# Inverse-FFT tail of a fused attention + spectral kernel: accumulating the second group's product in PSUM, stores ahead of loads on the SP queue, turned rows eight partitions apart

## The chip, the cores and the metric

The kernel runs on one core of one Trainium2 chip. The metric is the device time of one execution in microseconds (us), lower is better. The time before the change is the median of three executions.

## The reference

The network interleaves two kinds of residual block, twice: attention, spectral filter, attention, spectral filter. All tensors are float32, with 2048 rows and 1024 columns.

```python
def _A_ref(x, wqkv, wo):                      # 32 heads of 32 columns
    qkv = (x @ wqkv).reshape(B, S, 3, H, Dh).transpose(2, 0, 3, 1, 4)
    q, k, v = qkv[0], qkv[1], qkv[2]
    p = softmax(einsum("bhqd,bhkd->bhqk", q, k) * Dh ** -0.5)
    return einsum("bhqk,bhkd->bhqd", p, v).transpose(0, 2, 1, 3).reshape(B, S, D) @ wo

def _B_ref(x, w_r, w_i):
    X = rfft2(x, axes=(-2, -1)) * (w_r + 1j * w_i)
    return irfft2(X, s=(S, D), axes=(-2, -1))

x = A_x
x = x + _A_ref(_layernorm(x), A_wqkv, A_wo)
x = x + _B_ref(_layernorm(x), B_w_r, B_w_i)
x = x + _A_ref(_layernorm(x), A_wqkv, A_wo)
x = x + _B_ref(_layernorm(x), B_w_r, B_w_i)
```

## The kernel before

`build` calls, for each of two layers, `attention` and then `spectral`. Here layer 0 and layer 1 mean these two passes. The change lies in the last two parts of `spectral`, which run once in each layer, so everything told below happens twice in one execution: about 1645 to 1857 us (layer 0, followed by the attention of layer 1) and about 3490 to 3710 us (layer 1, followed by nothing).

`spectral` computes the two-dimensional FFT, the product with the weights and the inverse FFT as chains of matmuls. Its middle part works on 32 *units* (`UNITS`, units 0 to 15 in group g = 0, units 16 to 31 in group g = 1; four column blocks each, in a few units five). For each unit i there are these steps:

- `fb(i)`: 12 matmuls (forward transform along the rows) into PSUM, then `restack` on ScalarE copies them into the tile B (L1115).
- `fc(i)`: 8 matmuls, then four VectorE products with the weights w (L1161 to L1164) and two GpSimd adds (L1168, L1169). At its end `loadw(i + 3)` issues the load of a later unit's weights from the SP queue (L1089), and the weights are prepared on GpSimd (L1101).
- `halves(i)`: a copy on ScalarE (L1179) and a subtraction on VectorE (L1180) that make the float16 tile H.
- `binv(i)`: 12 matmuls with H, then `restack` into U on ScalarE.
- `cinv(i)`: 8 matmuls with U (L1199), a ScalarE copy into T, a tile with three buffers (L1204), and a *store* of T, 256 KB, to `zt[i]` in DRAM from the SP queue (L1205).
- `turn(i)` for even i: a *load* of 512 KB from `zt[i:i + 2]` back into SBUF, from the SP queue (L1209). It exchanges partitions and columns: two units make 16 rows of 64 x 128 float32, each row is one partition of the tile `turned`. `row(i, r, j)` says which partition a row lies in; the 16 rows of a turn are neighbours, `8 * (i % 16)` to `8 * (i % 16) + 15`. The constant matrix `mi` is laid out by the same function.

The loop over i runs 36 iterations as a software pipeline: iteration i does `fb(i)`, `halves(i - 2)`, `fc(i - 1)`, `binv(i - 3)`, for odd i from 7 on `turn(i - 7)`, then `cinv(i - 4)`, then for odd i the load of 128 rows of y, 512 KB, into `rest` (L1235). In this loop the order of the instructions on TensorE, ScalarE and SP is the order in which they are written (`manual_schedule`); the other engines, and everything where no such block stands, are ordered by the framework's planner. After the loop comes `turn(30)`. A turn waits for the stores of its two units. All of these DMAs are issued from one queue, SP, in order: an instruction there that waits holds up whatever stands behind it.

The last part applies the remaining inverse transform of length 16 and adds the result to the residual. For each of eight column blocks a, `even(a)` multiplies group 0 (`ai(a, 0)`, 8 matmuls of 128x128x128 float32, L1248, in the trace 16 instructions) and `odd(a)` multiplies group 1 (`ai(a, 1)`). Call the products p0 and p1, each a PSUM tile of two banks; four such tiles exist (`pq`). The residual has two halves, x0 and x1, and the result is x0 + p0 + p1 and x1 + p0 - p1. Before the change this is done so: ScalarE copies p0 to an SBUF tile e (L1257), VectorE adds p0 to x0 (L1258), VectorE subtracts p1 from e (L1265), VectorE adds p1 to x0 (L1266), GpSimd adds e to x1 (L1267). For the last block a = 7 one half of the columns is done by VectorE alone (L1274). The order is even(0) to even(3), then odd(0), even(4), odd(1), even(5), and so on.

In layer 0 this part also runs the first weight preparations of the next attention (`nxt`): eight loads of 256 KB from SP (L312), splits on ScalarE and VectorE (L218, L219) for v and on ScalarE and GpSimd (L321 to L323) for k and q. It also computes statistics for the coming layernorm (L1288, and `tile_root` in the middle of block 7). The next attention starts with a normalisation on ScalarE (L380) whose scale and bias come from `tile_root`. In layer 1 each finished block a is stored to the output, 1 MB each (L1292, and L1295 in two halves for the last).

Of the kernel before, what the change touches and what calls it, by code (L numbers as in the profile page):

```python
# [6 lines left out]
F32 = mybir.dt.float32  # L7
# [4 lines left out]
AF = mybir.ActivationFunctionType  # L12
ALU = mybir.AluOpType
# [9 lines left out]
UNITS = [u for g in range(2) for u in  # L23
         [(g, k1, list(range(4 * h, 4 * h + 4))) for k1 in range(1, 8) for h in range(2)]
         + [(g, k1, [0, 1, 2, 3] if g else [1, 2, 3, 0, 4]) for k1 in (0, 8)]]
# [4 lines left out]


def row(i, r, j):
    return 8 * (i % 16) + 2 * j + r


def spec_consts():
# [74 lines left out]
NG, NCH, NKT, NST = 8, 4, 16, 6  # L111
# [9 lines left out]
def ln_pow(nc, sm, cst, mv, eng, n=1):  # L121

    v, r = (sm.tile([128, n], F32, name=f"{c}{n}") for c in "vr")
    eng.tensor_scalar(v, mv[:, 1::2], 1e-5, None, op0=ALU.add)
    nc.gpsimd.tensor_tensor(r, v, cst["mhalf"].broadcast_to([128, n]), op=ALU.pow)
    return v, r


def ln_root(nc, sm, mv, v, r, eng, m=1.0):

    q, s, b = (sm.tile([128, 1], F32, name=f"{c}1") for c in "qsb")
    eng.scalar_tensor_tensor(q, r, r, v, op0=ALU.mult, op1=ALU.mult)
    eng.scalar_tensor_tensor(s, q, -3.0, r, op0=ALU.add, op1=ALU.mult)
    last = eng.scalar_tensor_tensor(b, mv[:, 0:1], 0.5 * m, s, op0=ALU.mult, op1=ALU.mult)
    eng.tensor_scalar(r, s, -0.5, None, op0=ALU.mult)
    return r, b, last
# [21 lines left out]
def tile_stats(nc, ap, flags, layer, t):  # L158
    if layer and t < NST:
        st = flags["st"][:, t]  # L160
        nc.vector.bn_stats(st[:, 1], ap.x[:, t, 512:1024])
    else:
        st = bn_stats(nc, ap.sm, ap.x[:, t])
    mv = flags["mv"][:, layer * 16 + t]
    nc.vector.bn_aggr(mv, st)
    return mv


def tile_root(nc, ap, cst, flags, layer, t):

    mv = tile_stats(nc, ap, flags, layer, t)
    v, r = ln_pow(nc, ap.sm, cst, mv, nc.vector)
    yield
    r, b, flags["pin"] = ln_root(nc, ap.sm, mv, v, r, nc.vector)
    flags["rb"] = r, b
    yield
# [827 lines left out]
def spectral(nc, tc, ap, yd, xout, a, cst, zt, fast, flags=None, nxt=None, join=None):  # L1004
# [25 lines left out]
    turned = ap.r.rearrange("p (g q n) -> p g q n", g=2, q=64)  # L1030
    rest = ap.big.rearrange("p (t d) -> p t d", d=1024)
    xo = rest.rearrange("p t (a u g q) -> p g a t u q", a=8, g=2, q=8)
# [84 lines left out]
    def complex_mm(out, lr, li, c):  # L1117

        sel = ((0, 0),) if parts == 1 else ((0, 0), (0, 1), (1, 0))
        mm_ = [(l[x], c[y][:, o:o + 256]) for l, o in ((lr, 128), (li, 0)) if l is not None for x, y in sel]  # L1120
        for k, (l, r) in enumerate(mm_):
            nc.tensor.matmul(out, l, r, start=k == 0, stop=k == len(mm_) - 1)  # L1122

    def const(n, k1):
        return [C[n][:, k1, y] for y in range(2)] if fast else [C[n][:, k1]]

    def new_ps(n):
        return [ps.tile([128, 2, 2, 128], F32, name="ps") for _ in range(2 if n == 5 else 1)]
# [47 lines left out]
    def halves(i):  # L1176
        while todo and todo[0][0] == i:
            _, gs, hi, lo = todo.pop(0)
            nc.scalar.copy(hi, gs)  # L1179
            nc.vector.tensor_sub(lo, gs, hi)  # L1180

    def binv(i):
        g, k1, fs = UNITS[i]
        n = len(fs)
        G = Gt.pop(i)
        pb = new_ps(n)
        for j, o, m in PAIRS[n]:
            lr, li = ([v[:, r, o:o + m].rearrange("p a f -> p (a f)") for v in G] for r in range(2))
            complex_mm(pb[j // 2][:64 * m, j % 2].rearrange("p r k -> p (r k)"), lr, li, const("cbi", k1))
        U = Ut[i] = p2.tile([128, 6, 128], F32, name="U")  # L1190
        restack(n, pb, U)

    def cinv(i):
        g, k1, fs = UNITS[i]
        n = len(fs)
        U = Ut.pop(i)
        pt = ps.tile([128, 4, 128], F32, name="ps")
        for j in range(4 if n == 4 else 3):
            nc.tensor.matmul(pt[:, j], C["ci"][:, 8 * g + fs[j]], U[:, j], start=True, stop=True)  # L1199
        if n == 5:  # L1200
            for j in range(2):
                nc.tensor.matmul(pt[64 * j:64 * j + 64, 3], C["ci"][:, 8 * g + fs[3 + j], 0:64], U[:, 4 + j], start=True, stop=True)
        t_ = p4.tile([128, 4, 128], F32, name="T")
        nc.scalar.copy(t_, pt)  # L1204
        nc.sync.dma_start(zt[i].rearrange("j p n -> p j n"), t_)  # L1205

    def turn(i):
        r0 = row(i, 0, 0)
        nc.sync.dma_start(turned[r0:r0 + 16, UNITS[i][0]],  # L1209
                          zt[i:i + 2].rearrange("i j (r q) n -> (i j r) q n", q=64))  # L1210

    for i in range(lead):
        loadw(i)
# [1 line left out]
    with tc.manual_schedule(engines=set(hold)) if fast else nullcontext():  # L1215
        for i in range(36):
            if i < 32:
                fb(i)
            if 0 <= i - 2 < 32 and fast:
                halves(i - 2)  # L1220
            if 0 <= i - 1 < 32:
                fc(i - 1)
            if 0 <= i - 3 < 32:
                binv(i - 3)
            if 7 <= i and i % 2:
                turn(i - 7)
            if 0 <= i - 4 < 32:
                cinv(i - 4)
            if i == 20 and join:
                joined = join(ps)  # L1230
            if 20 <= i < 23 and join:
                next(joined, None)
            if i % 2 and i < 32:
                t = i // 2
                nc.sync.dma_start(rest[:, t], yd[t * 128:(t + 1) * 128, :])  # L1235
        turn(30)
    psum.close()
    work.close()
    mid.close()
# [2 lines left out]
    psum = Pools(tc, None)  # L1242
    pq = psum("ai_ps", 4, space=PSUM)

    def ai(a, g):
        p = pq.tile([128, 8, 128], F32, name="ai")
        for q in range(8):
            nc.tensor.matmul(p[:, q], turned[:, g, 8 * a + q], cst["mi"][:, g], start=True, stop=True)  # L1248
        return p.rearrange("p q (t u) -> p t u q", u=8)

    def even(a):
        p = ai(a, 0)
        e = ap.pp.tile([128, 8, 128], F32, name="e", tag="p")
        ev = e.rearrange("p q (t u) -> p t u q", u=8)
        x0 = xo[:, 0, a]
        h = 8 if a < 7 else 4
        nc.scalar.copy(e[:, :h], p.rearrange("p t u q -> p q (t u)")[:, :h])  # L1257
        nc.vector.tensor_add(x0[:, :, :, :h], x0[:, :, :, :h], p[:, :, :, :h])  # L1258
        return p, e, ev

    def odd(a, p0, e, ev):
        p = ai(a, 1)
        x0, x1 = xo[:, 0, a], xo[:, 1, a]
        h = 8 if a < 7 else 4
        nc.vector.tensor_sub(e[:, :h], e[:, :h], p.rearrange("p t u q -> p q (t u)")[:, :h])  # L1265
        nc.vector.tensor_add(x0[:, :, :, :h], x0[:, :, :, :h], p[:, :, :, :h])  # L1266
        nc.gpsimd.tensor_tensor(x1[:, :, :, :h], x1[:, :, :, :h], ev[:, :, :, :h], op=ALU.add)  # L1267
        if a == 7:
            m, k = (iter(()), 8) if flags is None else (tile_root(nc, ap, cst, flags, 1, 0), 1)
            with tc.manual_schedule(engines={mybir.EngineType.DVE}):  # L1270
                for t in (slice(0, k), slice(k, 16)):
                    for n, (v, y, op) in enumerate(((x0, p0, ALU.add), (x1, p0, ALU.add), (x0, p, ALU.add),
                                                    (x1, p, ALU.subtract))):
                        nc.vector.tensor_tensor(v[:, t, :, h:], v[:, t, :, h:], y[:, t, :, h:], op=op)  # L1274
                        if n == (1 if t.start else 3):
                            next(m, None)

    first = [even(a) for a in range(4)]
    for a in range(8):
        odd(a, *first.pop(0))  # L1280
        if a < 4:
            first.append(even(a + 4))
        if nxt is not None:
            for _ in range(2):
                next(nxt, None)
            if 4 <= a < 4 + NST // 2:
                for t in range(2 * a - 8, 2 * a - 6):
                    nc.vector.bn_stats(flags["st"][:, t, 0], ap.x[:, t, 0:512])  # L1288
        else:
            sl = slice(a * 128, a * 128 + 128)  # L1290
            if a < 7:
                nc.sync.dma_start(xout[:, sl].rearrange("(t p) d -> p t d", p=128), ap.x[:, :, sl])  # L1292
            else:
                for t, q in ((0, nc.sync), (8, nc.scalar)):
                    q.dma_start(xout[t * 128:t * 128 + 1024, sl].rearrange("(t p) d -> p t d", p=128), ap.x[:, t:t + 8, sl])  # L1295
    if nxt is not None:
        run(nxt)
    psum.close()
# [224 lines left out]
```

## Time and profile before

| what | value |
|---|---|
| time, median of 3 executions | 3707.57 us (3706.04 to 3711.98) |
| time of the profiled execution | 3711.67 us |
| its span, first to last instruction | 3709.8 us |
| TensorE busy | 3606.5 us (97%) |
| VectorE busy | 3128.7 us (84%) |
| ScalarE busy | 2899.0 us (78%) |
| GpSimd busy | 664.0 us (18%) |
| 32 units of layer 0, first `fb` to last store | about 1645 to 1808 us |
| last part of layer 0 (L1248 to the next attention's first L380) | 1801 to 1856 us |
| last part of layer 1 | 3645 to 3710 us |

The busy shares are averages over the whole span, of which the spectral parts are about a tenth. Rows of the profile name an engine (PE is TensorE, PEld its weight loads, DVE VectorE, ACT ScalarE, POOL GpSimd, SPq the SyncE queue), a line of the kernel, the operation and the tiles. Since SBUF is swapped between the layers, `turned` and `rest` appear under the names of the buffers they lie in: in layer 0 `turned` is R and the residual is big, in layer 1 `turned` is big and the residual is R.

### The profile page before, as it was taken

The page shows a single profiled execution, that of the slowest core. Times are in us where ns is not written, and L with a number is a line of the kernel's source. Part 1 is how long each engine was busy: PE and PEld are TensorE (multiplying, and loading weights), DVE is VectorE, ACT ScalarE, POOL GpSimd, SP SyncE. Part 2 cuts the span into 40 slices and gives each one's busy share as a digit, 9 for nine tenths or more (in the row PEclk, how much of TensorE's full clock was granted, in tenths as well). Part 3 has the DMA queues.
Part 4 walks back from the last instruction along what each step waited for, and adds up shares of the span by engine and source line. Part 5 has one row for each costly group of instructions (what it writes and reads, how often), then busy time and mean ns, then how long its engine had stood idle before and what let it go on. Part 6 is the DMA issues. An engine that isn't in the chain of part 4 may idle for free.

```text
span 3709.8 us, 80239 instructions
## 1 busy us (share of the span) xinstructions
PE 3606.5 (97%) x32663; PEld 1595.9 (43%) x32663; DVE 3128.7 (84%) x3754; ACT 2899.0 (78%) x3571; POOL 664.0 (18%) x802
## 2 busy tenths in 40 slices
PE   8999999999999999999699999999999999999995
PEld 5333433343343333388663334334433433333895
DVE  7799899989998989886558998999899889788754
ACT  5788888888888967768448888888888888686783
POOL 1022112211221110024410111111111111000243
PEclk9999999999999999999899999999999999999998
DMA  7122232222232442139651232223222334322497
GB/s 198 21 53 54 52 55 52 56 47 55 47 64 54 97 109 78 69 129 209 151 162 22 55 60 49 55 48 61 41 53 55 64 58 99 100 77 74 137 213 185
DMA packets 238283, 307.71 MB, mean 83 GB/s; under 512 B 77392, under 2 KB 156752, under 8 KB 236368
## 3 DMA queue, kind: packets, MB, share of 16 engines
q1 hardware_dynamic: 198944, 228.49, 22.3%
q0 software_dynamic: 37632, 73.43, 13.7%
q8 instruction: 257, 4.21, 0.5%
q14 instruction: 122, 1.00, 0.1%
q10 hardware_dynamic: 1328, 0.59, 0.1%
HBM read 165.65 MB, written 135.20 MB: 81 GB/s over the span
## 4 chain that ended last, share of the span: by engine, by line
PE 84%; DVE 4%; DMA 4%; issue 4%; ACT 3%; POOL 1%; SPq 0%; DVEq 0%; ACTq 0%; POOLq 0%
PE o L746 24%; PE s L736 20%; PE x L426 16%; PE x L484 7%; PE x L547 6%; PE s L547 3%; DMA zt<-T 2%; PE ps L1122 2%; PE ps L1053 1%; PE ps L1038 1%; DVE acc L759 1%; PE ai L1248 1%; PE o L426 1%; DMA w<-in_w 1%; PE ps L1154 1%
## 5 line engine op out<-in xcount | busy, mean ns | idle before, releaser
L740 ACT ACTIVATE p<-s,bias 128x1024 f32<-128x1024 f32 x2048 | 2169.0, 1111 | 460.1 <-PE s L736 440.8
L759 DVE TENSOR_TENSOR acc<-acc,p 128x1024 f32<-128x1024 f32 x896 | 1044.6, 1223 | 55.8 <-ACT p L740 54.8
L759 DVE TENSOR_TENSOR big<-big,p 128x1024 f32<-128x1024 f32 x448 | 522.7, 1222 | 38.3 <-ACT p L740 37.1
L759 DVE TENSOR_TENSOR R<-R,p 128x1024 f32<-128x1024 f32 x448 | 522.5, 1223 | 31.4 <-ACT p L740 30.0
L746 PE MATMUL o<-p,R 128*32 128x512 f32 x4096 | 492.6, 598 | 0.0
L746 PE MATMUL o<-p,big 128*32 128x512 f32 x4096 | 492.5, 598 | 0.0
L426 PEld LDWEIGHTS <-wqk 128*128 128x128 f16 x3072 | 275.6, 98 | 419.8 <-issue 127.2
L426 PE MATMUL x<-R,wqk 128*128 128x512 f16 x1440 | 338.1, 381 | 1.9 <-ACT big L488 1.2
L426 PE MATMUL x<-big,wqk 128*128 128x512 f16 x1440 | 338.3, 381 | 1.4 <-ACT R L488 0.7
L736 PEld LDWEIGHTS <-R 32*128 32x128 f16 x6144 | 115.2, 93 | 370.5 <-issue 313.0
L736 PEld LDWEIGHTS <-big 32*128 32x128 f16 x6144 | 114.6, 93 | 370.3 <-issue 312.5
L746 PEld LDWEIGHTS o<-p,R 128*32 128x32 f32 x4096 | 107.2, 109 | 261.5 <-issue 261.5
L746 PEld LDWEIGHTS o<-p,big 128*32 128x32 f32 x4096 | 107.1, 109 | 261.5 <-issue 261.5
L736 PE MATMUL s<-R 32*128 32x512 f16 x3072 | 214.1, 378 | 0.1
L736 PE MATMUL s<-Q,big 32*128 32x512 f16 x3072 | 212.8, 378 | 1.0 <-DVE mqk L460 1.0
L736 PE MATMUL s<-Q,R 32*128 32x512 f16 x3072 | 212.7, 378 | 1.0 <-DVE mqk L460 1.0
L736 PE MATMUL s<-big 32*128 32x512 f16 x3072 | 212.8, 378 | 0.5 <-ACT p L740 0.4
L765 POOL DMA_DIRECT2D zd<-acc x112 | 92.3, 825 | 658.5 <-DVE z L775 308.6
L484 PE MATMUL x<-wv,big 128*128 128x256 f16 x1392 | 165.4, 275 | 3.2 <-DVE R L219 2.2
L484 PEld LDWEIGHTS <-big 128*128 128x128 f16 x1536 | 145.4, 98 | 49.1 <-issue 28.9
L484 PE MATMUL x<-wv,R 128*128 128x256 f16 x1392 | 165.7, 275 | 0.7 <-ACT R L392 0.7
L484 PEld LDWEIGHTS <-R 128*128 128x128 f16 x1536 | 145.6, 98 | 46.8 <-issue 26.1
(524 smaller groups left out, 4139.3 us busy)
## 6 DMA issues: line engine op xcount, KB each, us to landing
zd<-acc POOLq DMA_DIRECT2D x112, 256.0 KB, 4.1
wst<-in_wp SPq DMA_DIRECT2D x96, 256.0 KB, 3.5
zt<-T SPq DMA_DIRECT2D x64, 256.0 KB, 8.8
w<-in_w SPq DMA_DIRECT2D x60, 256.0 KB, 7.1
zd<-R POOLq DMA_DIRECT2D x56, 256.0 KB, 4.2
zt<-zr SPq DMA_DIRECT2D x224, 64.0 KB, 2.6
od<-ohl SPq DMA_DIRECT2D x56, 256.0 KB, 2.4
zd<-big POOLq DMA_DIRECT2D x56, 256.0 KB, 4.1
```

The source lines that it names most:

```text
L426: nc.tensor.matmul(ps, a, b, start=i == 0, stop=i == 23)
L484: nc.tensor.matmul(ps[:, j], x[c][:, d, o:o + 128], w[:, n, d], start=i == 0, stop=i == 23)
L547: nc.tensor.matmul(p, a, b, start=start and d == ds[0] and i == 0, stop=stop and d == ds[-1] and i == 2)
L736: nc.tensor.matmul(s[h // 2][:, h % 2], K[g][r, a, kt * 128:kt * 128 + 128], Q[g][r, b, c * 512:c * 512 + 512], start=i == 0, stop=i == 2)
L740: nc.scalar.activation(p, s[hf], AF.Exp, bias=bias[g], scale=SCALE / (SQ * SQ))
L746: nc.tensor.matmul(O[g, c][32 * h:32 * h + 32], V[g][:, kt, 32 * h:32 * h + 32], P[g, c, kt, h // 2][:, h % 2], start=kt == 0, stop=kt == ...
L759: last_add = nc.vector.tensor_add(a, a, p)
L765: nc.gpsimd.dma_start(z, a[32 * j:32 * j + 32].rearrange("p a j n -> p (a j n)"), max_dma_last_dim=2048, **({"accum_op": ALU.add} if j els ...
L1038: nc.tensor.transpose(pt[:, j], xv[:, g, :, 4 * i + j], ident)
L1053: nc.tensor.matmul(pa[:, j], tt[:, x, j], mm[:, g, y], start=k == 0, stop=k == 2)
L1122: nc.tensor.matmul(out, l, r, start=k == 0, stop=k == len(mm_) - 1)
L1154: nc.tensor.matmul(pc[:, j].rearrange("p r f -> p (r f)"), B[:, POS[n][o + j]], C["cc"][:, 8 * g + fs[o + j]], start=True, stop=True)
```

## The change

It has five parts.

1. `row` places the 16 rows of a turn eight partitions apart: turn i goes to partitions c, c + 8, ..., c + 120 with c = i % 16 // 2. `mi` follows by the same function.
2. In the loop `cinv(i - 4)` is written ahead of `turn(i - 7)`, so that on SP the store of unit i - 4 stands ahead of the turn. With the last iterations: before, SP has turn 26, store 29, store 30, turn 28, store 31, turn 30; after, it has store 29, turn 26, store 30, store 31, turn 28, turn 30.
3. `odd(a)` accumulates onto the PSUM tile of `even(a)` instead of using one of its own. Only the first matmul in each bank starts an accumulation. `even(a)` now only makes e = 2 p0 on ScalarE and adds it to x1 on GpSimd. `odd(a)` is two VectorE operations on p = p0 + p1: x0 += p and x1 -= p. The separate treatment of half of block 7 is gone.
4. TensorE and VectorE follow the written order in the last part: even(0) to even(3), odd(0), odd(1), even(4), odd(2), even(5), odd(3), even(6), odd(4), even(7), odd(5), odd(6), odd(7).
5. The first loads and splits of the next attention's weights (those called at a = 0) are issued only after `turn(30)`.

```diff
 def row(i, r, j):
-    return 8 * (i % 16) + 2 * j + r
+    return 8 * (8 * (i % 2) + 2 * j + r) + i % 16 // 2
...
     def turn(i):
         r0 = row(i, 0, 0)
-        nc.sync.dma_start(turned[r0:r0 + 16, UNITS[i][0]],
-                          zt[i:i + 2].rearrange("i j (r q) n -> (i j r) q n", q=64))
+        return nc.sync.dma_start(turned[r0:r0 + 121:8, UNITS[i][0]],
+                                 zt[i:i + 2].rearrange("i j (r q) n -> (i j r) q n", q=64))
...
             if 0 <= i - 3 < 32:
                 binv(i - 3)
+            if 0 <= i - 4 < 32:
+                cinv(i - 4)
             if 7 <= i and i % 2:
                 turn(i - 7)
-            if 0 <= i - 4 < 32:
-                cinv(i - 4)
...
-        turn(30)
+        back = turn(30)
...
+    tiles = {}
+
     def ai(a, g):
-        p = pq.tile([128, 8, 128], F32, name="ai")
+        if g == 0:
+            tiles[a] = pq.tile([128, 8, 128], F32, name="ai")
+        p = tiles[a]
         for q in range(8):
-            nc.tensor.matmul(p[:, q], turned[:, g, 8 * a + q], cst["mi"][:, g], start=True, stop=True)
+            nc.tensor.matmul(p[:, q], turned[:, g, 8 * a + q], cst["mi"][:, g], start=g == q % 4 == 0, stop=True, skip_group_check=True)
         return p.rearrange("p q (t u) -> p t u q", u=8)
 
     def even(a):
         p = ai(a, 0)
         e = ap.pp.tile([128, 8, 128], F32, name="e", tag="p")
-        ev = e.rearrange("p q (t u) -> p t u q", u=8)
-        x0 = xo[:, 0, a]
-        h = 8 if a < 7 else 4
-        nc.scalar.copy(e[:, :h], p.rearrange("p t u q -> p q (t u)")[:, :h])
-        nc.vector.tensor_add(x0[:, :, :, :h], x0[:, :, :, :h], p[:, :, :, :h])
-        return p, e, ev
+        nc.scalar.activation(e, tiles[a], AF.Copy, scale=2.0)
+        x1 = xo[:, 1, a]
+        nc.gpsimd.tensor_tensor(x1, x1, e.rearrange("p q (t u) -> p t u q", u=8), op=ALU.add)
 
-    def odd(a, p0, e, ev):
+    def odd(a):
         p = ai(a, 1)
...
+        m, k = (iter(()), 8) if flags is None else (tile_root(nc, ap, cst, flags, 1, 0), 1)
+        for t in (slice(0, k), slice(k, 16)) if a == 7 else (slice(0, 16),):
+            for x, op in ((xo[:, 0, a, t], ALU.add), (xo[:, 1, a, t], ALU.subtract)):
+                nc.vector.tensor_tensor(x, x, p[:, t], op=op)
+                if a == 7 and (t.start or op == ALU.subtract):
+                    next(m, None)
+
+    with tc.manual_schedule(engines={mybir.EngineType.PE, mybir.EngineType.DVE}):
+        for a in range(4):
+            even(a)
+        for a in range(8):
+            odd(a)
+            if 1 <= a < 5:
+                even(a + 3)
+            if nxt is not None:
+                with tc.issue_after(back.ins) if a == 0 else nullcontext():
+                    for _ in range(2):
+                        next(nxt, None)
...
```

What is left out of the loop over a (statistics in layer 0, output stores in layer 1) is the same as before.

More of the change, by code (lines that the diff above doesn't have):

```diff
@@ L1253, in even @@
         e = ap.pp.tile([128, 8, 128], F32, name="e", tag="p")
-        ev = e.rearrange("p q (t u) -> p t u q", u=8)
-        x0 = xo[:, 0, a]
-        h = 8 if a < 7 else 4
-        nc.scalar.copy(e[:, :h], p.rearrange("p t u q -> p q (t u)")[:, :h])
-        nc.vector.tensor_add(x0[:, :, :, :h], x0[:, :, :, :h], p[:, :, :, :h])
-        return p, e, ev
-    def odd(a, p0, e, ev):
-        p = ai(a, 1)
[L1263 to L1292, printed above, removed]
-            else:
-                for t, q in ((0, nc.sync), (8, nc.scalar)):
-                    q.dma_start(xout[t * 128:t * 128 + 1024, sl].rearrange("(t p) d -> p t d", p=128), ap.x[:, t:t + 8, sl])
+        nc.scalar.activation(e, tiles[a], AF.Copy, scale=2.0)
@@ new lines, in spectral @@
+    with tc.manual_schedule(engines={mybir.EngineType.PE, mybir.EngineType.DVE}):
[9 more added lines that the diff above has]
+                        next(nxt, None)
+                if 4 <= a < 4 + NST // 2:
+                    for t in range(2 * a - 8, 2 * a - 6):
+                        nc.vector.bn_stats(flags["st"][:, t, 0], ap.x[:, t, 0:512])
+            else:
+                sl = slice(a * 128, a * 128 + 128)
+                if a < 7:
+                    nc.sync.dma_start(xout[:, sl].rearrange("(t p) d -> p t d", p=128), ap.x[:, :, sl])
+                else:
+                    for t, q in ((0, nc.sync), (8, nc.scalar)):
+                        q.dma_start(xout[t * 128:t * 128 + 1024, sl].rearrange("(t p) d -> p t d", p=128), ap.x[:, t:t + 8, sl])
```

## The prediction

> **What bounds the kernel now.** I read the page first, then the chain of work in the two windows around the change, then the order of the SP queue there, then the rows of single operations.
>
> ```profile
> span 3709.8 us, 80239 instructions
> PE 3606.5 (97%) x32663; PEld 1595.9 (43%) x32663; DVE 3128.7 (84%) x3754; ACT 2899.0 (78%) x3571; POOL 664.0 (18%) x802
> ```
>
> Over the whole span TensorE is the bound, so work saved on VectorE counts only where TensorE stands still. The chain of layer 0, then that of layer 1 (start, length, what):
>
> ```profile
> 1781.38 7.71 DMA w<-in_w
> ...
> 1807.59 6.88 DMA zt<-T
> 1814.48 7.06 DMA R<-zt
> 1821.90 12.58 PE ai L1248 x96
> ...
> 3619.49 9.35 DMA zt<-T
> ...
> 3653.38 6.74 DMA zt<-T
> 3660.18 6.50 DMA big<-zt
> 3667.04 13.28 PE ai L1248 x96
> ```
>
> In both layers the end of the loop is a row of transfers: a store lands, the turn that needs it goes out, behind the turn the next store (3653.38), behind that the last turn. Group 1 of the last part starts at L = 1821.90 and at L = 3667.04. When the arithmetic was done, and what SP did, shows the timeline (start, length, engine, line; in brackets the idle time before and its releaser):
>
> ```profile
> 1800.52 0.94 PE L1199 MATMUL ps<-U,ci 128*128 128x128 f32 x6 [0.28 <-ACT U L1115]
> 1801.29 7.31 PE L1248 MATMUL ai<-mi,R 128*128 128x128 f32 x64
> 1801.72 0.58 ACT L1204 COPY T<-ps 128x512 f32<-128x512 f32 x1 [0.65 <-DMA zt<-T]
> 1807.17 0.32 SPq L1209 DMA_DIRECT2D R<-zt  x1
> 1807.59 0.38 SPq L1205 DMA_DIRECT2D zt<-T  x1
> 3644.41 0.94 PE L1199 MATMUL ps<-U,ci 128*128 128x128 f32 x6 [0.28 <-ACT U L1115]
> 3648.47 0.59 ACT L1204 COPY T<-ps 128x512 f32<-128x512 f32 x1 [2.02 <-DMA zt<-T]
> ```
>
> The last unit's matmuls end at 1801.46 and 3645.35. In layer 0 its T is ready at 1802.30, but its store goes out at 1807.59: on SP it stands behind turn 28 (1807.17), which waits for store 29. That is the wait that the change takes out.
>
> **The change part by part.** First the durations of the transfers, by issues in windows where little else moved (line, count, KB, us to landing), and all stores of layer 1:
>
> ```profile
> w<-in_w SPq DMA_DIRECT2D x3, 256.0 KB, 2.7
> big<-y SPq DMA_DIRECT2D x2, 512.0 KB, 3.7
> big<-zt SPq DMA_DIRECT2D x1, 512.0 KB, 6.5
> DMA to landing us min/median/max: 2.8/9.4/11.5
> ```
>
> *Stores ahead of turns.* After the change SP has store 29, turn 26, store 30, store 31, turn 28, turn 30. Store 31 then follows its T copy at once. In layer 0: matmuls end 1801.46, copy 0.58, T ready 1802.1. Its landing lies between 2.8 (the least, alone) and 6.88 (behind a turn); I take 4.0, as turn 26 and store 30 are just ahead of it and the turn behind. Turn 30 goes out 0.1 later. Behind a wait on SP now stand the turn and the y load, which wait for the T copy ahead of them; nothing needs either within those few us, so this costs nothing while no turn but the last two is near the end.
>
> *Rows eight partitions apart.* The last turn moved 512 KB with nothing beside it and took 6.5; 512 KB of y over all 128 partitions took 3.7. The number of bytes is the same, the difference is 16 neighbouring partitions. So after the change a turn lies between 3.7 and 6.5; I take 4.6, nearer to the spread load. [...] Turn 30 also has turn 28 ahead of it, for which I add 0.9: 5.5 in all.
>
> *The loop before.* Two forward products of neighbouring units on TensorE, where the loop runs freely:
>
> ```profile
> 1671.78 1.47 PE L1122 MATMUL ps<-cb,big 128*128 128x256 f16 x12
> 1676.18 1.47 PE L1122 MATMUL ps<-cb,big 128*128 128x256 f16 x12
> ```
>
> A unit takes TensorE 4.4, a pair 8.8. In that time SP's queue carries a turn, two stores, a y load and two w loads, 2 MB, and is nearly full: a w load that takes 2.7 alone took 7.71 on the chain above. Shorter turns shorten that queue, and the last unit's weights arrive earlier. What this gives is between 0 and 5.0 (7.71 - 2.7) in each layer; I take 2.0, since TensorE waited little in the loop, here in layer 0 from 1660 to 1801 (the idle time stands behind the second bar):
>
> ```profile
> L1122 PE MATMUL ps<-cbi,H 128*128 128x256 f16 (+1 forms) x372 | 48.3, 276 | 6.7 <-DVE H L1180 3.4 <-ACT H L1179 3.3
> ```
>
> So L in layer 0: 1802.1 - 2.0 + 0.1 + 4.0 + 0.1 + 5.5 = 1809.8, that is 12.1 earlier. In layer 1: 3645.35 + 0.58 + 0.1 = 3646.0, less 2.0, plus the same 9.7: 3653.7, 13.3 earlier. The four evens, 7.31 by the row above, end at 1806.8 and 3650.7, so they lie beside the transfers and cost nothing; if the transfers took under 7.3 they would be the next limit.
>
> **After L.** These rows give the pieces:
>
> ```profile
> 1825.56 1.22 DVE L1265 TENSOR_TENSOR e<-e,ai 128x1024 f32<-128x1024 f32 x1 [8.55 <-PE ai L1248]
> 1829.53 1.21 DVE L1265 TENSOR_TENSOR e<-e,ai 128x1024 f32<-128x1024 f32 x1
> 1830.66 1.22 DVE L1266 TENSOR_TENSOR big<-big,ai 128x1024 f32<-128x1024 f32 x1
> 1834.40 2.91 POOL L1267 TENSOR_TENSOR big<-big,e 128x1024 f32<-128x1024 f32 x1 [0.68 <-DVE e L1265]
> 1846.61 1.28 DVE L1288 BATCH_NORM_STATS2 fst<-big 128x6 f32<-128x512 f32 x2
> 1856.46 1.52 ACT L380 ACTIVATE xn<-big,b,r 128x512 f32<-128x512 f32 x2 [17.81 <-DVE r L135]
> 1810.82 1.29 DVE L219 SCALAR_TENSOR_TENSOR wv<-wst,wv 128x512 f16<-128x512 f32 x2
> ```
>
> Before, VectorE did three operations of 1.14 (1829.53 to 1830.66) for a block, 3.4 us, and from 1825.56 on it was the limit; from L to the next attention's first activation passed 1856.46 - 1821.90 = 34.6. After, it does two, 2.3 us, against two products of 7.31 / 4 = 1.83 on TensorE. The number of matmuls and of ScalarE and GpSimd operations stays. Now e goes to GpSimd right after the even product, so its 2.9 lies beside the transfers for blocks 0 to 3. The new wait is even(4), whose PSUM tile is free only when VectorE has finished odd(0): odd(0) at 1.83, VectorE to 4.2, then even(4); odd(4) ends at 15.3, odd(7) at 22.6 after L. VectorE has after L: odd(0) to (3) with four splits of 0.65 to 14.0, then, each waiting for TensorE or following on, odd(4) 15.3 to 17.7, statistics 1.3, odd(5) and statistics to 22.6, odd(6) and statistics to 26.3, then the first slice of block 7, its statistics, one long operation and the root, 3.2: 29.5. I count odd(0) at 1.83, not at the 3.66 of 1821.90 to 1825.56: TensorE stood still 13 us there and 3 us after the change, and the granted clock fell to half only later than that:
>
> ```profile
> 1810.00:1811.00 1.00, 0.00 (x0) 0.00 (x0) 1.00 (x2) 0.69 (x2) 0.00 (x0) 1.00 0.01 1
> 1812.00:1813.00 1.00, 0.00 (x0) 0.00 (x0) 0.10 (x1) 0.00 (x0) 0.00 (x0) 0.50 0.83 122
> ```
>
> (The third number from the end is the clock; the evens had ended at 1808.6.) If the clock falls after all, it costs 1.8 a layer.
>
> *Splits beside GpSimd.* The splits L219 read two SBUF tiles, and GpSimd will now be adding e at that time. A like pair in the loop:
>
> ```profile
> 1792.41 0.73 POOL L1168 TENSOR_TENSOR G<-G,t__21510 128x256 f32<-128x256 f32 x1 [0.60 <-DVE t__21510 L1162]
> 1792.52 1.17 DVE L1180 TENSOR_TENSOR H<-G,H 128x512 f16<-128x512 f32 x1
> 1795.51 0.69 DVE L1180 TENSOR_TENSOR H<-G,H 128x512 f16<-128x512 f32 x1 [1.37 <-ACT H L1179]
> ```
>
> L1180 took 1.17 beside the GpSimd operation and 0.69 without: it lost most of that operation's rest. Four splits could lose from 0 to 4 x 2.9 = 11.6; VectorE has waits of about 1 to absorb, and I take a net 2.0. [...]
>
> So layer 0: 29.5 + 2.0 = 31.5 instead of 34.6, 3.1 gained. The moved loads of weights (first issue about 1804.8) are there when the first split is due, 4.2 after L = 1814.0, by the page's median of 3.5 with several us to spare; that is their cover:
>
> ```profile
> wst<-in_wp SPq DMA_DIRECT2D x96, 256.0 KB, 3.5
> ```
>
> Layer 1 ends with the output stores:
>
> ```profile
> 3675.03 22.43 SPq L1292 DMA_DIRECT2D out<-R  x7
> 3703.00:3706.00 3.00, 0.00 (x0) 0.00 (x0) 0.00 (x0) 0.00 (x0) 0.00 (x0) 0.50 1.05 294
> 3706.00:3707.00 1.00, 0.00 (x0) 0.00 (x0) 0.00 (x0) 0.00 (x0) 0.00 (x0) 0.50 0.69 196
> ```
>
> The DMA engines are full to the end (share 1.05, 294 GB/s, then nothing after 3707). 8.39 MB at 294 take 28.5, and they took 31.7 from the first issue. So what counts is when the first store can go: 8.0 after L before, 4.2 after; 3.8, of which I count 3.7. Blocks then come every 3.7, later every 2.3, against 3.6 for a store, so the gap at the start shrinks; of 3.2 I count 1.0. Sum 4.7.
>
> **Sum.** 12.1 + 3.1 + 13.3 + 4.7 = 33.2. Against the profiled execution, 3711.67, that gives 3678.5; that execution stands 4.1 above the median 3707.57, so I forecast 3707.6 - 33.2 = 3674.
>
> **Rivals.**
> *Spreading the rows gives nothing.* The limit could be the 16 rows themselves. Then each turn stays at 6.5: L is later by 1.9 for the turn and about 1.0 for the one ahead, and the 2.0 of the loop is lost, 5 a layer: gain 23, 3684. For it: rows of 32 KB stay rows of 32 KB. Against: 3.7 for the same bytes.
> *The queue empties altogether.* Stores land at 2.8 (1.2 less), turns at 3.7 (0.9 and about 0.9 for the one ahead), the loop gives 4 (2.0 more): 5 more a layer, gain 43, 3664. For it: the minima of the rows. Against: three transfers still go out together at the end.
> *The splits hold VectorE.* All four are held for 2.9 by GpSimd, or the first waits as long for a load behind turn 30: 11.6 instead of 2.0, some 9 more in layer 0, gain 24, 3683. [...] Against: GpSimd rests between its adds.
> *Slower: the stepped rows run on fewer DMA engines or in smaller pieces.* Then a turn fills its queue longer. In the 8.8 of a pair there move besides a turn 1.5 MB, 5.3 at the 294 GB/s above, an estimate. So a turn has some 3.5 of pure transfer before the loop is bound by it; today it has, 2.8 more than y's 512 KB (1.8 at 294), about 4.5. Each further us costs 16 a layer, 32 in all, and from about 1 us over today's the gain is gone. At half the engines, 9 us, it would be some 110 slower: 3820. [...]
>
> **How the numbers follow.** The forecast has 0.54, no gain from spreading 0.18, the empty queue 0.14, held splits 0.09, slower 0.03, and 0.02 for a gain that is lost elsewhere. The range from 3661 to 3689 takes in the first four with their bounds and leaves out about 0.1 to 0.15. A difference of 0.2%, 7.4 us, is about what measurements of this kernel can tell from none. All but the last two are faster: 0.95 faster, 0.02 same, 0.03 slower.
>
> **What would show it.** Turns to landing under 5.5 at the end of each layer; store 31 within 0.2 of its T copy; L1248 of group 1 at about 1810 - and, with layer 0's gain of 15, at about 3638 in layer 1; no idle over 4 before it; L1265 and L1258 gone, about 31 from L to L380; the first output store 4.2 after L and stores full to the end. Wrong would make it: turns of 6.5 or more, VectorE waiting at L219, ScalarE holding an e behind a weight that has not landed, or even(4) waiting more than 1 us for its PSUM tile.

## The result, and the profile after

The changed kernel takes 3678.07 us (median of 4 runs, 3676.38 to 3679.55), the kernel before beside it 3707.61 (4 runs, 3706.04 to 3711.98): a ratio of 0.9918 with a 95% interval of 0.9901 to 0.9936, 29.5 us less. The forecast was 3674, its range 3661 to 3689. The profiled execution of the changed kernel took 3676.38, the fastest of the four; that of before, 3711.67, was near the slowest of its own. So the two traces lie 35.3 apart, 5.8 more than the medians.

From the page of the changed kernel, the span, the engines and the transfers from SP (count, KB, us to landing):

```profile
span 3674.6 us, 80167 instructions
...
PE 3600.5 (98%) x32663; PEld 1589.4 (43%) x32663; DVE 3104.2 (84%) x3726; ACT 2903.9 (79%) x3571; POOL 674.7 (18%) x802
...
zt<-T SPq DMA_DIRECT2D x64, 256.0 KB, 3.9
w<-in_w SPq DMA_DIRECT2D x60, 256.0 KB, 3.1
```

TensorE does the same 32663 matmuls in nearly the same busy time; what went is idle time. A store of T lands in 3.9 (8.8 before), a load of unit weights in 3.1 (7.1 before), though the size and shape of neither was edited: they share the queue with the turns, and the stores now stand ahead of them. With the rows alone (an experiment below) it is 5.3 and 3.0. All turns, from issue to landing (6.5/8.9/10.4 before):

```profile
DMA to landing us min/median/max: 4.7/6.4/7.5
```

The chain of work at the end of layer 1 (start, length, what):

```profile
3626.55 3.99 DMA zt<-T
3630.59 4.98 DMA big<-zt
3635.91 2.04 PE ai L1252 x16
3638.03 2.36 DVE R L1267 x2
3640.53 14.54 PE ai L1252 x128
```

Before, the last store took 6.74 and the last turn 6.50, and ahead of them stood a wait for an earlier store of 9.35. Now the last store takes 3.99 and goes out 0.02 after its copy, the last turn takes 4.98, and the earlier store is off the chain. Layer 0 by the timeline (start, length, engine, line; in brackets the idle time before and its releaser):

```profile
1798.74 1.40 SPq L1205 DMA_DIRECT2D zt<-T  x2
1799.81 7.41 PE L1252 MATMUL ai<-mi,R 128*128 128x128 f32 x64 [0.72 <-ACT T L1204]
1800.24 4.07 SPq L1209 DMA_DIRECT2D R<-zt  x2
1809.48 3.81 PE L1252 MATMUL ai<-mi,R 128*128 128x128 f32 x32 [2.26 <-DMA wst<-in_wp]
1811.60 2.35 DVE L1267 TENSOR_TENSOR big<-big,ai 128x1024 f32<-128x1024 f32 x2 [16.43 <-ACT wv L218]
1814.10 7.38 PE L1252 MATMUL ai<-mi,R 128*128 128x128 f32 x64 [0.81 <-DVE big L1267]
1816.97 3.94 DVE L219 SCALAR_TENSOR_TENSOR wv<-wst,wv 128x512 f16<-128x512 f32 x2
1840.89 1.52 ACT L380 ACTIVATE xn<-big,b,r 128x512 f32<-128x512 f32 x2 [9.96 <-DVE r L135]
```

Both stores go out one right behind the other, then both turns; group 1 starts at 1809.48 (1821.90 before), after 2.26 us of idle TensorE where there had been 13.3. The bracket names a weight load as releaser, but a product does not read weights: it is the turn, issued at 1803.84, which lands 5.51 later, at 1809.35. even(4) waits 0.81 for its PSUM tile.

Where the 35.3 went, in the profiled pair. "Loop" is from the first `fb` product of a layer to the last `cinv` product, "end" from there to L:

| stretch | before | after | gain |
|---|---|---|---|
| loop, layer 0 / layer 1 | 157.42 / 155.49 | 155.38 / 153.39 | 2.0 / 2.1 |
| end of the loop to L, layer 0 / layer 1 | 20.45 / 21.70 | 10.39 / 10.06 | 10.1 / 11.6 |
| L to the next attention's L380 | 34.56 | 31.41 | 3.2 |
| L of layer 1 to the end | 42.8 | 38.7 | 4.1 |
| all else (attention and what lies ahead) | | | 2.2 |

### The profile page after: what moved, and what is told of

The parts are those of the page before. It is cut to its first block, busy times and chain, and to the rows that moved or that the text cites. A ratio compares the mean times of both kernels' runs of the same rounds, so it can differ in the third digit from the quotient of the medians.

```text
span 3674.6 us, 80167 instructions
## 1 busy us (share of the span) xinstructions
PE 3600.5 (98%) x32663; PEld 1589.4 (43%) x32663; DVE 3104.2 (84%) x3726; ACT 2903.9 (79%) x3571; POOL 674.7 (18%) x802
```

## The experiments

The same stages in every kernel (loop, end of the loop to L, L to the next attention, L to the first output store; one profiled execution each). With the loop's code as before it came out at 157.4/155.5 in one and 155.1/152.3 in another, so 2 or 3 us there are no evidence by themselves. The medians are from several sessions, in which the kernel before had 3707.6 to 3709.6; differences under 2 us between them tell nothing.

| kernel | median | loop 0 / 1 | end 0 / 1 | to L380 | to store |
|---|---|---|---|---|---|
| before | 3707.6 | 157.4 / 155.5 | 20.5 / 21.7 | 34.6 | 8.0 |
| rows alone | 3688.1 | 152.9 / 148.9 | 17.6 / 12.3 | 35.4 | 7.9 |
| order alone | 3698.5 | 155.6 / 153.8 | 13.9 / 16.4 | 37.9 | 8.0 |
| rows and order | 3687.2 | 155.5 / 153.4 | 10.6 / 10.1 | 37.4 | 6.3 |
| last part alone | 3703.7 | 155.1 / 152.3 | 20.1 / 22.7 | 32.9 | 6.2 |
| changed, rows undone | 3688.4 | 155.7 / 152.1 | 14.6 / 16.3 | 31.2 | 6.2 |
| changed, rows two apart | 3677.6 | 155.7 / 152.0 | 9.4 / 10.8 | 31.8 | 5.5 |
| changed, order undone | 3677.4 | 154.5 / 149.0 | 11.3 / 12.5 | 32.9 | 5.9 |
| changed, three adds out (one run) | 3677.9 | 155.9 / 153.4 | 11.1 / 10.2 | 30.2 | 5.2 |
| **the change** | 3678.1 | 155.4 / 153.4 | 10.4 / 10.1 | 31.4 | 4.5 |
| changed, order late | 3674.0 | 154.5 / 148.9 | 9.5 / 10.1 | 32.5 | 4.5 |
| order late, last turn split | 3673.4 | 155.3 / 148.9 | 9.7 / 10.0 | 32.6 | 5.9 |

**Each part alone.** To the kernel before, only the rows:

```diff
-    return 8 * (i % 16) + 2 * j + r
+    return 8 * (8 * (i % 2) + 2 * j + r) + i % 16 // 2
-        nc.sync.dma_start(turned[r0:r0 + 16, UNITS[i][0]],
+        nc.sync.dma_start(turned[r0:r0 + 121:8, UNITS[i][0]],
```

> The kernel before with the rows of a turn eight partitions apart and nothing else. Theory A (the turns were slow because of where their rows lay, and everything behind them on the queue with them): the last turns land in 4.5 to 5.5 us instead of 6.5 to 7.1, the stores that stand behind a turn in 4.5 instead of 6.8, the loop is 2 us shorter in each layer as in the changed kernel, group 1 starts about 11 us earlier than before in each layer, about 24 us in all: 3684. Theory B (the order of stores and turns on SP carries the gain, the rows little): turns stay above 6.5, no more than 5 us in all: 3703.

Measured 3688.08 (3687.05 to 3689.77), ratio 0.9947 (0.9935 to 0.9959): 20 us less than before, where theory A had 24. So the rows do most of it, in the loop of layer 1 (148.9, a larger gain than the 2 expected) and in its end (21.7 to 12.3). In layer 0 the end stays long, and there the last turn took 6.19 instead of 4.5 to 5.5. Store 31 had landed 6.4 after its issue, at 1806.6, but SP has three weight loads ahead of the last turn:

```profile
1800.18 0.53 SPq L1205 DMA_DIRECT2D zt<-T  x1
1800.77 8.42 SPq L312 DMA_DIRECT2D wst<-in_wp  x3
1809.28 0.48 SPq L1209 DMA_DIRECT2D R<-zt  x1
```

Only the order:

```diff
-            if 7 <= i and i % 2:
-                turn(i - 7)
             if 0 <= i - 4 < 32:
                 cinv(i - 4)
+            if 7 <= i and i % 2:
+                turn(i - 7)
```

> The kernel before with the stores written ahead of the turns and nothing else. Theory A: the last store goes out right behind its copy, 5.3 us earlier in layer 0, but it and the last turn still land slowly; the loop is not shorter; group 1 starts 5 to 6 us earlier in each layer, about 11 in all: 3697. Theory B: about 10 in each layer, 20 or more in all: 3687 or less.

Measured 3698.5 (3696.6 to 3699.99), 0.9973 (0.9963 to 0.9983): 10 less. The last turns still take 7.5 and 7.2, but one transfer fewer stands in the row. Both edits together:

> Both parts on the transfers, with the old last part (VectorE makes three passes over each block). Theory A: the two parts overlap, since a turn that is short leaves little for a store to wait behind: group 1 starts at about 1809.5 in layer 0 as in the changed kernel, the first activation of the next attention comes about 33 to 34 us after it; in all about 27 us faster than before: 3681, so that rows alone give most of it. If the parts simply add up (rows 24, order 11): 35, 3673.

Measured 3687.23 (3686.73 to 3689.41), 0.9945 (0.9933 to 0.9957): 21 less, where rows alone gave 20 and order alone 10. The two remove the same wait, and the expectation of 3681 underrated that: what follows L grew to 37.4, because with a short wait the old last part has more VectorE work left after L (32.7 busy between L and L380, 28.7 before), and the loop of layer 1 grew from 148.9 to 153.4. That second number is taken up below.

The new last part alone (parts 3 to 5 of the change):

> The new last part alone (accumulation in PSUM, written order of TensorE and VectorE, weight loads behind the last turn), with the old rows and the old order on SP. Theory A: group 1 starts as late as before (about 1821.9 in layer 0); TensorE stands still for 13 us and runs its first product at half the clock as before; behind it the layer 0 part takes 33 instead of 34.6, the first output store comes 6.3 instead of 8.0 after group 1 starts: about 4 us in all: 3704, hardly to be told from no change. Theory C (fewer VectorE passes are where the gain comes from): 3 VectorE operations of 1.14 become 2 for each of 16 blocks, 18 us: 3690.

Measured 3703.66 (3700.38 to 3708.4), 0.999 (0.9981 to 0.9999): 5 less, so theory C falls. Which of parts 3, 4 and 5 carries it was not tested apart. Alone it starts group 1 on a TensorE that has stood still for 13 us. Its first products in the timeline, and the windows there (third number from the end: the granted clock):

```profile
1820.34 5.51 PE L1252 MATMUL ai<-mi,R 128*128 128x128 f32 x32 [12.95 <-DMA R<-zt]
```

```profile
1820.00:1822.00 2.00, 1.66 (x8) 1.69 (x9) 0.00 (x0) 1.10 (x2) 0.00 (x0) 0.50 0.51 196
```

The same 32 matmuls take 5.51 at clock 0.50, and 3.81 in the changed kernel at 1.00. On top of rows and order the last part gives 3687.2 - 3678.1 = 9.2, twice as much: from L to L380 37.4 becomes 31.4, to the first store 6.3 becomes 4.5. Most of the difference is in layer 0, where L to L380 shrinks by 6.0 instead of 1.7. Of these 4.3, 2.8 come from the old last part, which grew from 34.6 to 37.4 as the wait ahead of it went, and 1.5 from the new one, which shrank from 32.9 to 31.4 with the clock at 1.00.

**Is it the spreading that makes turns short?** The changed kernel with neighbouring rows again, and with rows two apart, all within 32 partitions:

```diff
-    return 8 * (8 * (i % 2) + 2 * j + r) + i % 16 // 2
+    return 32 * (i % 16 // 4) + 2 * (8 * (i % 2) + 2 * j + r) + i % 4 // 2
...
-        return nc.sync.dma_start(turned[r0:r0 + 121:8, UNITS[i][0]],
+        return nc.sync.dma_start(turned[r0:r0 + 31:2, UNITS[i][0]],
```

> The changed kernel with the 16 rows of a turn in neighbouring partitions again. Theory A (the distance of the rows carries most): the last turns land in 7.0 to 7.5 again, group 1 starts at about 1814.4 and 9 us after the evens in layer 1, as in the run of the order alone; about 14 us slower than the changed kernel: 3692. Rival from the prediction (spreading gives nothing): the time of the changed kernel, 3678.

> The changed kernel with the rows of a turn two partitions apart instead of eight, so that they lie within 32 partitions. [...] Theory Q (rows must be spread over all 128 partitions): turns between 5.6 and 7, and a time between 3682 and 3692.

Neighbouring: 3688.37 (3687.34 to 3689.45), 0.9944 (0.9927 to 0.996). Two apart: 3677.57 (3675.85 to 3680.79), 0.9916 (0.9899 to 0.9932). The last turn of layer 1 in the chain of each, first neighbouring, then two apart:

```profile
3638.21 7.62 DMA big<-zt
```

```profile
3630.12 5.68 DMA big<-zt
```

The rows are worth 10.3 on top of the rest (14 expected), so the rival that spreading gives nothing falls. Rows over a quarter of the partitions give the same time as rows over all of them. Their last turns, 5.64 and 5.68, lie in the range of theory Q, but over all 32 turns they take 5.2/6.5/7.5 (least, median, longest), eight apart 4.7/6.4/7.5, neighbouring 7.4/8.5/10.8. The packets in the traces show it more directly, as each row of a turn is one DMA packet of 32 KB. Its median time over the 512 rows is 3.6 us in the kernel with neighbouring rows (3.7 in the kernel before), 2.1 with rows eight apart and 2.2 with rows two apart. It isn't the width that counts, then. Why rows in neighbouring partitions take longer was not shown.

**Do GpSimd's adds hold the splits?** The changed kernel without GpSimd's add for blocks 4, 5 and 6 in layer 0 (so their part of x1 is left out):

```diff
-        nc.gpsimd.tensor_tensor(x1, x1, e.rearrange("p q (t u) -> p t u q", u=8), op=ALU.add)
+        if flags is None or not 4 <= a < 7:
+            nc.gpsimd.tensor_tensor(x1, x1, e.rearrange("p q (t u) -> p t u q", u=8), op=ALU.add)
```

> The changed kernel, but in layer 0 GpSimd's addition of e to x1 is left out for blocks 4, 5 and 6, so that the last three splits of weights on VectorE (L219) meet no addition of that kind. [...] Theory H (they wait for their weights to land): nothing changes.

The group of splits in the window from 1808 to 1842, changed kernel and this one (busy, mean ns of one, idle before):

```profile
L219 DVE SCALAR_TENSOR_TENSOR wv<-wst,wv 128x512 f16<-128x512 f32 x4 | 6.0, 1514 | 0.0
```

```profile
L219 DVE SCALAR_TENSOR_TENSOR wv<-wst,wv 128x512 f16<-128x512 f32 x4 | 2.7, 684 | 0.0
```

With the adds gone the splits are back at 684 ns, so theory H falls: the adds hold them, for 3.3 in all. The mean hides how: in the changed kernel the four took 0.91, 0.68, 3.34 and 1.13. Three began while an add ran and ended 0.55 after that add did; the third began at 1817.57, 0.31 into an add that ran until 1820.36, and ended at 1820.91. The second began in a rest of GpSimd and lost nothing. From L to L380 it took 30.2 instead of 31.4, 1.2 less. The clock took back some of the gain: in this execution it fell to 0.50 at 0.95 after L, which is 1810.84 here, and the first 32 products took 5.44 instead of 3.81.

```profile
1811.00:1812.00 1.00, 1.00 (x9) 1.00 (x9) 0.00 (x0) 0.85 (x2) 1.00 (x2) 0.90 0.20 74
1812.00:1813.00 1.00, 1.00 (x7) 1.00 (x6) 0.00 (x0) 0.96 (x2) 1.00 (x2) 0.50 0.00 0
```

Counted from VectorE's first operation after L, past odd(0), it is 1840.89 - 1811.60 = 29.3 with the adds and 1841.04 - 1813.81 = 27.2 without: 2.1, at unequal clocks. The one time taken, 3677.9, is no different from the changed kernel's.

**What the order does to the loop.** With the spread rows, the loop of layer 1 takes 148.9 where the turn stands ahead of the store, and 153.4 in the changed kernel. Nearly all of it is one place: around iteration 24 two forward products of neighbouring units are 8.84 apart instead of 4.42. The timeline of the changed kernel there:

```profile
3570.33 0.18 PE L1428 MATMUL ps<-sign,fa 6*1 6x1 f32 x2
...
3570.55 0.15 DVE L1430 TENSOR_SCALAR fb<-ps 1x1 f32<-1x1 f32 x1 [4.24 <-PE ps L1428]
3570.80 0.40 DVE L1161 TENSOR_TENSOR G<-ps,w 128x256 f32<-128x256 f32 x1
...
3573.81 0.62 ACT L1179 CAST H<-G 128x512 f16<-128x512 f32 x1 [4.90 <-POOL G L1169]
...
3574.48 0.39 PE L1122 MATMUL ps<-cbi,H 128*128 128x256 f16 x2 [1.66 <-ACT H L1179]
```

L1430 belongs to a small test of flags that the loop interleaves (`join`, iterations 20 to 22). It waits 4.24 for its matmul, and all the products of a unit stand behind it on VectorE; then GpSimd, ScalarE and TensorE wait in turn. TensorE and SP follow the written order here, VectorE does not: the planner places its instructions, and moving a DMA on SP was enough for it to put L1430 ahead. This wait of L1430 (another line number in some), 4.24, stands in each of the kernels here with the new order in the whole loop, with either rows, and in none with the old one; the two products there are 8.7 to 8.9 apart in four of them and 7.25 in the other two. So the new order where it is needed and the old one elsewhere:

```diff
+            if 7 <= i < 31 and i % 2:
+                turn(i - 7)
             if 0 <= i - 4 < 32:
                 cinv(i - 4)
-            if 7 <= i and i % 2:
+            if 31 <= i and i % 2:
                 turn(i - 7)
```

> The changed kernel, but the stores stand ahead of the turns only in the last iterations of the loop (from 31 on); before that the old order holds. Theory J (the new order, through the planner, moved an operation on VectorE that waits for TensorE ahead of other work, and this costs one stall of 4.3 us in iteration 24 of layer 1 and about 2 us in layer 0): that stall goes, the loops take 153 and 149 instead of 155.4 and 153.4, the drain stays as short as in the changed kernel; about 6 us faster than the changed kernel: 3672. Theory K (the order of stores and turns within the loop matters by itself): 3678 or more.

Measured 3674.04 (3673.26 to 3675.68), 0.9905 (0.9889 to 0.9922): 4.0 less than the changed kernel, where theory J had 6. The stall went as it said; the loop of layer 0 gained 0.9 instead of 2, and in layer 0 the clock fell to 0.50, so that L380 came 32.5 after L instead of 31.4. The same operation there, now L1432:

```profile
3574.33 0.41 DVE L1164 TENSOR_TENSOR t__42554<-ps,w 128x256 f32<-128x256 f32 x1
3574.66 0.13 DVE L1432 TENSOR_SCALAR fb<-ps 1x1 f32<-1x1 f32 x1
```

It stands behind the unit's products and waits for nothing; the loop of layer 1 takes 148.9. And the order undone everywhere:

> The changed kernel with part 2 undone everywhere: the turn stands ahead of the store on SP again, in the loop and at its end; rows eight apart, accumulation, written order and the late weight loads stay. Theory O (what the order gives at the end of the loop is bought back by the VectorE order that it brings into the loop): loops of 153 and 149 us as in the kernel with the spread rows alone, from the last unit's copy to group 1 about 17.6 less the loads that no longer stand ahead of the last turn, 14 to 16, in layer 0 and 12 in layer 1, against 10.4 and 10.0; sum about 3677 to 3680, that is the same as the changed kernel within 2 us: the order everywhere is worth nothing net. Rival (the order is worth the 10 us that it gave alone): 3685 to 3688.

Measured 3677.39 (3676.38 to 3679.59), 0.9913 (0.99 to 0.9927), the same as the changed kernel. In the changed kernel the order as a whole is thus worth nothing: 0.9 and 2.4 at the ends of the two loops, against 4.4 in the loop of layer 1 and 0.9 in that of layer 0. In these two executions another 1.5 and 1.4 lie behind L (32.9 against 31.4, 5.9 against 4.5), since with the old order TensorE idled 4.1 and 5.3 ahead of L and the clock fell to 0.50. The expectation had 14 to 16 for the end in layer 0; 11.3 was measured, because the new last part leaves nothing on SP between store 31 and the last turn:

```profile
1798.93 0.51 SPq L1205 DMA_DIRECT2D zt<-T  x1
1804.02 0.48 SPq L1209 DMA_DIRECT2D R<-zt  x1
1804.67 1.41 SPq L312 DMA_DIRECT2D wst<-in_wp  x3
```

**Can the last turn be shortened?** The version with the late order, rows four apart, and the last turn as two of one unit each:

```diff
-        return nc.sync.dma_start(turned[r0:r0 + 121:8, UNITS[i][0]],
-                                 zt[i:i + 2].rearrange("i j (r q) n -> (i j r) q n", q=64))
+        return nc.sync.dma_start(turned[r0:r0 + 32 * n - 3:4, UNITS[i][0]],
+                                 zt[i:i + n].rearrange("i j (r q) n -> (i j r) q n", q=64))
...
-        back = turn(30)
+        turn(30, 1)
+        back = turn(31, 1)
```

> The kernel with stores ahead of turns only from iteration 31 on (3674.0), with two more edits: the last turn is issued as two turns of one unit each (256 KB, 8 rows), unit 30's ahead of that of unit 31, and the rows of a turn lie four partitions apart within a half of the partitions. Theory H (the last turn's time goes with the bytes that wait for store 31, and half of them can go as soon as store 30 has landed): the last turn lands 3.3 to 4.0 after its issue instead of 4.8 to 5.6, group 1 starts 1 to 1.5 us earlier in each layer, bounded by the 2.3 and 2.9 us that TensorE stands idle ahead of it; 3671 to 3672. [...]

Measured 3673.37 (3667.58 to 3674.11), 0.9896 (0.9881 to 0.9911), which can't be told from 3674.04. The chain of layer 1:

```profile
3622.93 4.47 DMA zt<-T
3627.41 4.54 DMA big<-zt
3632.19 3.44 PE ai L1255 x16
```

The half turn takes 4.54, hardly less than 4.79 for the whole turn in the version with the late order, so theory H falls. The packets in the trace show how: the two halves go as two waves of eight packets, the first starting from 3628.05 on, the second only from 3629.81 on, when the first is through. The sixteen packets of the whole turn in the version with the late order start within 0.7 of each other. So the half that needs store 31 stood behind the half that did not. And the first 16 matmuls of group 1 took 3.44 here, 2.04 in the changed kernel, as the clock had gone to 0.50.

## Why the prediction was right, step by step

| step | predicted | measured in the profile |
|---|---|---|
| store 31 to landing | 4.0 | 4.00 and 3.99 |
| turn 30 to landing | 5.5 | 5.51 and 4.98 |
| loop, gain in each layer | 2.0 | 2.0 and 2.1 |
| L in layer 0 | 1809.8 | 1809.48 |
| gain ahead of L, layer 0 / layer 1 | 12.1 / 13.3 | 12.1 / 13.7 |
| L to L380 | 31.5 | 31.4 |
| of it, what the held splits cost | 2.0 | about 2.1 |
| L to the first output store | 4.2 | 4.5 |
| gain after L in layer 1 | 4.7 | 4.1 |
| idle TensorE ahead of L | under 4 | 2.26 and 2.91 |
| even(4) waits for PSUM | under 1 | 0.81 and 0.80 |

The mechanism held, and so did most places where the text said what would be seen. One did not: the last turns were to land in under 5.5 and took 5.51 and 4.98, those just ahead of them 6.12 and 6.43. The sum of 33.2 stands against 35.3 in the profiled pair, 1.8 of the difference being the attention of layer 1, which no edit touches, and against 29.5 between the medians.

Four things in it were not as put.

First, *the loop*. "Shorter turns shorten that queue" is right, but 2.0 is a balance of two terms that the text did not have: with the spread rows and the old order the loop of layer 1 takes 148.9, which is 3.4 to 6.6 less than the 152.3 and 155.5 seen with neighbouring rows, so the upper bound of 5.0 was too low against the profile of before; and the new order takes up to 4.4 back through L1430. With the new order the rows give the loop of layer 1 nothing (153.4 with them, 152.1 without), and their 10.3 lie at the two ends, 4.2 and 6.3. The prediction named what stands behind a wait on SP, and said that the turn's new place costs nothing. On SP that was so; on VectorE, whose order the planner remakes, it cost a wait of 4.24.

Second, *the order*. The prediction calls the store's place behind turn 28 the wait that the change takes out. With spread rows that wait is short by itself: undoing the order lengthens the ends only from 10.4 to 11.3 and from 10.1 to 12.5, so what took the wait out was mostly the rows.

Third, *the clock*. It counted on a warm clock behind 3 us of idle TensorE, from windows of before; there the clock fell at 1811.6, 3.0 after the evens had ended. The close agreement behind L (31.4 for 31.5, 4.5 for 4.2) is from an execution in which the clock did not fall in either layer, after 2.26 and 2.91 of idle time; in other versions it fell after 2.31 and 2.54 (last section), so this could not be counted on. Where it fell, L380 came 32.5 after L (order late), and the first store 5.2 to 5.9 (three adds out, rows two apart, last turn split).

Fourth, *the offset*. The sum was made on an execution of before that stands 4.1 above the median, and subtracted from the median; the result is 4.1 above the forecast. But that execution had one of the longest loops (157.4 and 155.5, against 155.1 and 152.3 where the same loop ran under the new last part), so part of what the change took away was probably not in the median to begin with. That a long loop is what set that execution apart is argued from two traces, not shown.

Of the rivals, no gain from spreading is refuted (10.3 on top of the rest, 20 alone), the slower turns of the last rival too. Held splits came in part: 3.3 of the 11.6, as three of the four met the rest of an add and one met none. The empty queue did not come: the last turns keep about 5, all turns 6.4 in the middle.

How the parts share the gain depends on the order of counting, since they work on one wait: rows 20 alone and 10 last, order 10 alone, 1 on top of the rows and nothing last, last part 5 alone and 9 last.

## What to carry to other kernels

Where two edits shorten the same chain of transfers, price them together and say which is left when the other is there: here the cheaper of the two, a swap of two lines, was worth 10 alone and nothing with the other. After moving an instruction on an engine whose order is written, look again at the engines whose order is planned, over the whole stretch that was edited and not only at its end. A wait that goes takes with it the cover for what ran beside it, and TensorE's clock can stay up without it (here 1.00 at the start of group 1, 0.50 with the wait), so what follows the wait is measured with the wait gone: here the new last part gave 5 before and 9 after.

## What the runs showed of the hardware

The granted clock did not fall after a fixed idle time. Ahead of group 1 TensorE idled 2.26 and 2.91 in the changed kernel, 2.48 and 2.93 in the one with rows and order, 2.91 in layer 1 of the version with the late order, and went on at full clock (32 matmuls in 3.81). It idled 2.31 in layer 0 of the version with the late order, 2.54 and 2.80 in the one with the split turn, 2.96 and 3.06 in the one without three adds, and the clock went to half between 0.5 ahead of L and 1.2 behind it (32 matmuls in 5.20 to 5.44).

The fall cost 1.4 to 1.6 for these 32 matmuls. What decides whether the clock falls was not shown: 2.31 was followed by a fall and 2.93 was not. Whether such falls are why the runs of the changed kernel differ by 3.2 us stays open.

The price of GpSimd's adds to the splits was 0.83 us for one split on average (1514 against 684 ns), from nothing to 2.66 for one. A DMA packet of 32 KB into one partition took 3.6 to 3.7 us in the median where the rows of a turn were neighbours, and 2.1 to 2.2 where they lay eight or two apart. Landing times of transfers whose own shape nobody edited fell with the rows alone from 8.8 to 5.3 (stores) and from 7.1 to 3.0 (weight loads), when one transfer in the queue got shorter.
